# Batch 0's keys kept once, and a new hand order: a block-sparse attention and hardswish kernel on one core

## The chip, the cores and the metric

The kernel runs on one core of a Trainium2 chip. The metric is the device time of one execution in microseconds. A NeuronCore has five engines that run side by side: TensorE (PE; its weight loads are listed as PEld), VectorE (DVE), ScalarE (ACT), GpSimd (POOL) and SyncE (SP). POOL and SP also issue DMAs.

## The reference

```python
batch, n_heads, seq, head_dim = (4, 8, 768, 64); block, window = (32, 16)
k_sum = k.reshape(B, H, nb, block, D).max(axis=3)       # 24 block maxima of the keys
v_sum = v.reshape(B, H, nb, block, D).mean(axis=3)
mask_l = np.abs(pos[:, None] - pos[None, :]) < window
scores_l = where(mask_l, scale * q @ k.T, -1e9)
scores_s = scale * q @ k_sum.T + np.log(block)
a = softmax(concatenate([scores_l, scores_s], axis=-1))
attn = a @ concatenate([v, v_sum], axis=2)
x = attn.transpose(0, 2, 1, 3).reshape(B * S, H * D)     # 3072 x 512
h = x @ w_in                                             # 512 x 2048
out = (h * clip(h + 3, 0, 6) / 6) @ w_out                # 2048 x 512
```

Inputs and output are float32. The kernel multiplies in bfloat16.

## The kernel before, in words

**Attention.** 64 queries (a "tile" t, 12 per head) see 96 neighbouring keys (`WIN`) and the 24 block maxima: 120 columns (`KEYS`). Two heads make a pair p, of which there are four (`NP`); j is the head of a pair, on partitions 0 to 63 or 64 to 127. For every tile the stationary operand of the scores is a 128-column slot of `kb` that holds its 96 keys, the 24 maxima and 8 zeros. Neighbouring windows overlap, so a key stands in two slots, and each pair's maxima stand in twelve. ACT takes the exponential, DVE multiplies the band mask, and the values are products of the exponentials (120 rows) with `vaug`: 64 rows of V, 32 rows of "halo" (the neighbour's rows), 24 block sums and a column of ones for the denominator.

**Batch 0** is done a pair at a time as it arrives: `load_k` and `load_q` (POOL, casting to bfloat16), `k_step` (sixteen transposes on PE, a DVE maximum `red`, copies into `kaug` for half 1 and half 0, a broadcast of the maxima), `q_step`, `scores`, `vsum_first` (block sums of V by products with the indicator `ind`), `halo`. Half 0 of a pair is tiles 6 to 11, half 1 tiles 0 to 5. **Batches 1 to 3** are loaded ahead (`load_raw`, `load_nat`) and transposed on DVE or by DMA; `scores_all`, `vsum` and `values_half` work on them.

**The FFN** works on eight token tiles s of 384 rows (two a batch): `f1` makes two of sixteen column blocks of w_in per step (8 matmuls of 384 columns), ACT and DVE turn them into g; `f2` multiplies g by w_out (16 matmuls for 128 rows), copies and stores. Its matmuls take most of TensorE's time.

**The order** of all engines is written out by hand in the string `ORDER`, in tokens such as `k01.2:A`: tag, step of that tag, engine. Tags: K, Q, V, I, O loads of K, Q, V, w_in, w_out (batch, part); k, q transposes and copies (batch, pair); s scores; u sums of V; h halos; v values; F and G steps of `f1` and `f2` (token tile, part); c, e, z, f constants; w the rest of the keys of a batch; y a two-element POOL copy that holds back loads. `Plan.run` walks the tokens, assigns buffers, and sorts by planned begin; each engine's queue then is in that order. Where it plans that PE will wait in the first 27 us (`WARM`), `keep` puts in filler matmuls of 512 columns (line 983) so that the clock stays up. PSUM is three pairs of banks "S" and two banks "h".

## Time and profile before

| | |
|---|---|
| median of 3 runs | 214.84 us (214.73 to 215.09) |
| the profiled execution | 214.44 us, of which the span is 212.7 |
| busy time of PE, DVE, ACT, POOL | 205.3, 149.8, 110.6, 66.9 us |
| filler matmuls of line 983 | 21, 8.2 us busy |
| DMA | 25.01 MB, 121846 packets |

A row of a timeline has the start, the time it took, the engine, the line, the operation, output and inputs, how many in a row, and in brackets the idle time before and what ended it. A row of a group has busy time and mean ns of one, then idle time before. A row of a window has the stretch, its length, busy time of PE, PEld, DVE, ACT and POOL with counts, the granted clock of TensorE, DMA share and GB/s. A DMA row has the issuing queue, count, size and median time from issue to landing.

### The profile page before, as it was taken

To read this page: it belongs to the slowest core of one execution; us is meant where nothing else is said; L and a number is where in the kernel's file an instruction comes from. 1 tells how busy PE (TensorE), PEld (TensorE's weight loads), DVE (VectorE), ACT (ScalarE), POOL (GpSimd) and SP (SyncE) were. 2 spreads that over 40 slices of the span, in tenths; PEclk is the share of its full clock that TensorE was granted. 3 is DMA by queue.
4 is the path that set the end of the run, shared out by engine and by line. 5 is a ranking of instruction groups with operands and counts; after the bars stand their busy time and mean duration, and the time that the engine had idled before them with its cause. 6 is when DMAs were issued, how large, how long until landed. Compare 5 with 4: busy or idle time off the path is not lost.

```text
span 212.7 us, 4928 instructions
## 1 busy us (share of the span) xinstructions
PE 205.3 (97%) x2105; PEld 116.8 (55%) x2105; DVE 149.8 (70%) x238; ACT 110.6 (52%) x157; POOL 66.9 (31%) x81
## 2 busy tenths in 40 slices
PE   7969999999999999999999999999999999999994
PEld 2447686655446555555555556555464555555462
DVE  5788988999978897898568679981874347542102
ACT  5478856658299036836893045669501246531120
POOL 7999247345420029945973000000000000000000
PEclk9988999999999999999999999999999999999999
DMA  4999999999999659999999999901109002000242
GB/s 64 184 157 194 179 135 177 147 149 184 151 115 47 176 123 103 143 210 153 162 148 143 136 190 171 208 0 52 51 3 197 0 3 99 0 0 3 99 159 89
DMA packets 121846, 25.01 MB, mean 118 GB/s; under 512 B 112864, under 2 KB 118880, under 8 KB 121824
## 3 DMA queue, kind: packets, MB, share of 16 engines
q0 software_dynamic: 102336, 14.47, 108.0%
q1 hardware_dynamic: 19488, 10.23, 20.4%
q8 instruction: 16, 0.26, 0.5%
q14 instruction: 6, 0.05, 0.1%
HBM read 28.93 MB, written 6.29 MB: 166 GB/s over the span
## 4 chain that ended last, share of the span: by engine, by line
PE 90%; DVE 6%; ACT 2%; issue 0%; ACTq 0%; DVEq 0%
PE S L868 39%; PE h L890 29%; PE S L890 11%; PE S L784 3%; PE h L983 2%; PE S L658 2%; DVE vaug L502 2%; ACT kb L502 1%; DVE xn L837 1%; DVE at L641 1%; DVE kb L544 1%; PE h L517 1%; PE S L694 1%; DVE q L502 1%; DVE red L538 0%
## 5 line engine op out<-in xcount | busy, mean ns | idle before, releaser
L868 PE MATMUL S<-x,win 128*128 128x384 bf16 (+1 forms) x544 | 88.3, 317 | 0.0
L874 ACT ACTIVATE r<-S 128x768 f32<-128x768 f32 x64 | 51.3, 811 | 67.2 <-PE S L868 65.6
L876 DVE SCALAR_TENSOR_TENSOR g<-r,S 128x768 bf16<-128x768 f32 x64 | 59.6, 948 | 26.8 <-ACT r L874 26.1
L868 PEld LDWEIGHTS <-win 128*128 128x128 bf16 x544 | 51.2, 98 | 34.8 <-issue 0.2
L890 PE MATMUL h<-wout,g 128*128 128x512 bf16 (+1 forms) x288 | 67.4, 370 | 0.0
L890 PEld LDWEIGHTS <-g 128*128 128x128 bf16 x416 | 38.4, 98 | 38.6
L890 PE MATMUL S<-wout,g 128*128 128x512 bf16 (+2 forms) x128 | 25.8, 346 | 0.0
L664 ACT ACTIVATE at<-S 120x1024 bf16<-120x1024 f32 x18 | 17.5, 1031 | 4.3 <-PE S L658 4.2
L453 POOL DMA_DIRECT2D vaug<-in_v_dram x16 | 15.2, 955 | 8.1 <-DMA wout<-in_moe_w_out_dram 4.3
L666 DVE TENSOR_TENSOR at<-at,mask 96x1024 bf16<-96x1024 bf16 x18 | 11.9, 685 | 7.4 <-ACT at L664 7.2
L442 POOL DMA_DIRECT2D nat<-in_q_dram x8 | 10.5, 1318 | 7.1 <-issue 7.1
L442 POOL DMA_DIRECT2D nat<-in_k_dram x8 | 10.7, 1348 | 5.0 <-issue 2.3
L502 ACT COPY ot<-h 128x512 f32<-128x512 f32 (+1 forms) x14 | 7.9, 567 | 7.3 <-PE h L890 5.2
L502 DVE COPY ot<-S 128x512 f32<-128x512 f32 (+2 forms) x6 | 3.5, 577 | 11.2 <-PE S L890 11.2
L719 DVE TENSOR_REDUCE red<-kb 128x48 bf16<-128x1536 bf16 x6 | 10.5, 1744 | 0.0
L502 DVE COPY vaug<-vs 24x768 bf16<-24x768 bf16 x17 | 6.0, 354 | 3.4 <-ACT vs L502 3.0
L784 PEld LDWEIGHTS <-at 120*64 120x64 bf16 x336 | 6.1, 111 | 2.7 <-issue 1.6
L983 PE MATMUL h<-g 128*128 128x512 bf16 x15 | 6.1, 566 | 1.5 <-DVE g L323 1.5
L792 DVE TENSOR_TENSOR xm<-S,rc 128x768 bf16<-128x768 f32 x8 | 7.5, 955 | 0.1
L596 DVE STREAM_TRANSPOSE kb<-nat 128x768 bf16<-128x768 bf16 x8 | 7.4, 957 | 0.0
L784 PE MATMUL S<-vaug,at 120*64 120x65 bf16 x336 | 7.0, 196 | 0.3 <-ACT vaug L502 0.3
L637 ACT ACTIVATE at<-S 120x768 bf16<-120x768 f32 x8 | 6.3, 818 | 1.8 <-PE S L628 1.7
(100 smaller groups left out, 161.4 us busy)
## 6 DMA issues: line engine op xcount, KB each, us to landing
out_dram<-ot SPq DMA_DIRECT2D x19, 256.0 KB, 2.5
vaug<-in_v_dram POOLq DMA_DIRECT2D x16, 192.0 KB, 8.0
win<-in_moe_w_in_dram POOLq DMA_DIRECT2D x4, 512.0 KB, 11.2
wout<-in_moe_w_out_dram POOLq DMA_DIRECT2D x4, 512.0 KB, 17.3
nat<-in_k_dram POOLq DMA_DIRECT2D x10, 192.0 KB, 13.1
nat<-in_q_dram POOLq DMA_DIRECT2D x10, 192.0 KB, 8.1
out_dram<-ot SPq DMA_DIRECT2D x4, 224.0 KB, 2.7
nat<-in_k_dram POOLq DMA_DIRECT2D x6, 128.0 KB, 7.0
```

The costliest lines, as they stand in the source:

```text
L442: op("POOL", 1.35, over=0.01, fn=lambda src=src, name=name, hs=hs, ds=ds, rows=rows: nc.gpsimd.dma_start(out=raw[b % 2][name][rows], in_=s ...
L453: op("POOL", 0.945, lambda: nc.gpsimd.dma_start(out=o[BLK:WIN, lo:hi, 0:D], in_=rows[:, lo:hi]), w=[("v", b % 2, c)], dma=1.28, els=1536)
L502: {"ACT": nc.scalar.copy, "DVE": nc.vector.tensor_copy, "POOL": nc.gpsimd.tensor_copy}[eng](o, i)
L664: op("ACT", 1.02, lambda: nc.scalar.activation(odds[0:KEYS, :, w], X.slot[0:KEYS], AF.Exp, scale=scl), r=[X], w=[("atg", k)])
L666: op("DVE", 0.69, lambda: nc.vector.tensor_tensor(odds[0:WIN, :, w].rearrange("p j (t c) -> p j t c", c=QB), odds[0:WIN, :, w].rearrange(" ...
L719: nc.vector.tensor_reduce(red.slot[:].rearrange("x (p u e n) -> x e u p n", p=NP, u=NS, e=2)[:, e], w[:, n * e:n * e + n, BLK:WIN].rearran ...
L784: nc.tensor.matmul(X.slot[64 * c:64 * c + 64, e, (D + 1) * y:(D + 1) * (y + 1)], at[p][0:KEYS, j, t * QB:(t + 1) * QB], vaug[b % 2][0:KEYS ...
L868: nc.tensor.matmul(h.slot[:, f, lo * 128:hi * 128].rearrange("p (u c) -> p u c", c=128), w_in_sb[:, kt, (ft + f) * 128:(ft + f + 1) * 128] ...
L874: op("ACT", 0.81, lambda: nc.scalar.activation(r.slot[:], h.slot[:, :, 0:HALF], AF.Relu, bias=0.5, scale=1.0 / 6.0), r=[h], w=[r], alloc=r)
L876: op("DVE", 0.955, lambda: nc.vector.scalar_tensor_tensor(gt[s].slot[:, ft:ft + 2], r.slot[:], 1.0, h.slot[:, :, 0:HALF], op0=ALU.min, op1 ...
L890: nc.tensor.matmul(bank(o)[:, a:z], gt[s].slot[:, ft, ts * 128:(ts + 1) * 128], w_out_sb[:, ft, a:z], start=(ft == 0), stop=(ft == NFT - 1))
L983: nc.tensor.matmul(o, idle[:, 0:128], idle[:], start=True, stop=True)
```

## The change

For batch 0 the keys of a pair are kept once: 32 halo columns, 768 keys in order, 24 maxima. A tile's 96 keys are a slice of it, and the maxima get two products of their own per half (384 columns, one for each head), into rows 96 to 119 of the same PSUM tile. The maximum is written straight into its place, and the copies write each key once. The queries of half 0 stay in the order in which they were loaded, and the products read them with a stride.

With it comes more. K of pairs 1 to 3 of batch 0 is loaded in float32 by SP and cast by ACT and DVE (`load_wide_k`). POOL makes its masks first, then loads Q, K of pair 0 and V, and only then the wide queries. The block sums of V of batch 0 are made for two pairs at a time. Batch 3's block sums no longer come from TensorE: POOL loads V once more, a block to a row (`load_blocks`), and DVE adds (`sum_blocks`). POOL may copy halos and block sums (`ANY`): it has three copies of halos (batches 0 and 1) and ten of block sums. `scores_all` takes its tiles by half instead of by pair, half 1 first. The second half of batch 1 is transposed by PE (twelve transposes) instead of by DMA. The order is written anew. There are 15 filler matmuls instead of 21.

```diff
-K01.0 K02.0 Q010.0 c.2 Q000.0 c.1 K00.0 k01.0 c.0 e.4 z2.0:D c.9 e.1 f.0 e.2 c.4 c.7 c.8 e.0 k01.1 k01.3:D z0.0:A z1.0:A
+K01.0 K02.0 c.0 c.8 f.0 c.2 c.1 c.3 Q000.0 K00.0 Q010.0 c.4 c.9 C01.0:D V00.0 V03.0 V01.0 z2.0:A C01.1:A z1.0:A z0.0:A z3.0:D
...
+    ANY = ("ACT", "DVE", "POOL")
-    kaug = [kb[0][:, p * NQ:(p + 1) * NQ] for p in range(NP)]
+    keys = [kb[0][:, p * NQ:(p + 1) * NQ].rearrange("x t c -> x (t c)")[:, 0:BLK + S + NB] for p in range(NP)]
...
+    def load_wide_k(b, lo, hi):
+        plan.at(f"K{b}{lo}")
+
+        def raw_(p, n):
+            at_ = 2 * (p - 1) * RUN * D
+            return hards[0][0:RP].rearrange("p f c -> p (f c)").bitcast(F32)[:, at_:at_ + n * RUN * D].rearrange("p (h s d) -> p h s d", h=n, s=RUN)
+        op("SP", 0.4, lambda: nc.sync.dma_start(out=raw_(lo, 2 * (hi - lo)), in_=k[b, 2 * lo:2 * hi].rearrange("h (p s) d -> p h s d", s=RUN)),
+           w=[("kf", p) for p in range(lo, hi)], dma=0.95 * (hi - lo), kind="load")
+        for p in range(lo, hi):
+            plan.at(f"C{b}{p}")
+            for j in range(2):
+                op(EITHER, {"ACT": 0.59, "DVE": 0.68}, lambda eng, p=p, j=j: copy(eng, knat[:, 2 * p + j], raw_(p, 2)[:, j]),
+                   r=[("kf", p)], w=[("kn", p, j)])
...
-            src = bass.AP(tb.tensor, x[:, 8 * t0 - 4, 0].offset, [list(tb.ap[0]), [8, t1 - t0], [1, WIN // RUN], [RP, RUN]])
-            copy(eng, f[:, t0:t1, 0:WIN].rearrange("p t (a s) -> p t a s", s=RUN), src)
+            x = bank(T).bitcast(BF16)[:, 0:S].rearrange("p (s r) -> p r s", s=RUN)
+            o = keys[p][:, 0:BLK + S].rearrange("p (r s) -> p r s", s=RUN)
+            n, m = BLK // RUN, HALF // RUN
             if half:
+                copy(eng, o[:, n:m], x[:, 0:m - n])
+                copy(eng, o[:, 0:n], x[:, RP - n:RP])
+            else:
+                copy(eng, o[:, m:RP + n], x[:, m - n:RP])
...
-        op("DVE", 0.24, over=0.03, fn=lambda: nc.vector.tensor_copy(kaug[p][:, :, WIN:KEYS], red.slot[:, 0:NB].unsqueeze(1).to_broadcast([128, NQ, NB])),
-           r=[red], w=[("km", p)])
...
+        def asks(rows, lo, hi):
+            if half:
+                return qT[1][rows, p, lo * QB:hi * QB]
+            return qT[0][rows, p].rearrange("p (s c) -> p c s", s=RUN // 2)[:, lo * RP // HQ:hi * RP // HQ]
+
         def mms():
+            for i in range(HQ):
+                t = low(half) + i
+                for j in range(2):
+                    rows = slice(64 * j, 64 * j + 64)
+                    nc.tensor.matmul(X[p, half].slot[0:WIN, j, i * QB:(i + 1) * QB], keys[p][rows, t * QB:t * QB + WIN],
+                                     asks(rows, i, i + 1), start=not masked, stop=not masked or i == HQ - 1)
+            for j in range(2):
+                rows = slice(64 * j, 64 * j + 64)
+                nc.tensor.matmul(X[p, half].slot[WIN:KEYS, j, 0:HALF], keys[p][rows, BLK + S:], asks(rows, 0, HQ), start=not masked, stop=True)
...
-    def vsum_first(c):
+    def vsum_first(cs):
...
             for t in range(NQ):
+                for i, c in enumerate(cs):
+                    nc.tensor.matmul(bank(T)[BLK * i:BLK * i + BLK, 0:2 * D], ind[:, t], vaug[0][0:WIN, 2 * c:2 * c + 2, t, 0:D],
+                                     start=(t == 0), stop=(t == NQ - 1))
...
+    def load_blocks(b, c):
+        plan.at(f"B{b}{c}")
+        op("POOL", 0.8, lambda: nc.gpsimd.dma_start(out=rows_v(b, c), in_=v[b, 2 * c:2 * c + 2].rearrange("h (n r) d -> n h (r d)", r=BLK)),
+           w=[("vb", b, c)], dma=0.95, els=192, free=[(n, 0, g) for n in ("Kr", "Qr") for g in range(4)])
+
+    def sum_blocks(b):
+        plan.at(f"U{b}")
+        vs, n = Buf("vs"), D // 2
+        for h in range(2):
+            for lo in (0, n):
+                def go(h=h, lo=lo):
+                    x = both[0][:].rearrange("p u m -> p (u m)")[:, h * BLK * D:(h + 1) * BLK * D].rearrange("p (r d) -> p d r", r=BLK)
+                    nc.vector.tensor_reduce(total[:, h * D + lo:h * D + lo + n], x[:, lo:lo + n], axis=AX.X, op=ALU.add)
+                op("DVE", 1.22, go, r=[("vb", b, c) for c in range(NP)], w=[("vp", b, h, lo)])
+        op(EITHER, {"ACT": 0.265, "DVE": 0.25}, lambda eng: copy(eng, vs.slot[:], total[:]), r=[("vp", b, h, lo) for h in range(2) for lo in (0, n)],
+           w=[vs], alloc=vs)
+        spread(b, vs)
...
-                op(EITHER, {"ACT": 0.83, "DVE": 0.37}, over=-0.02, fn=lambda eng, c=c, x=x: copy(
+                op(ANY, {"ACT": 0.83, "DVE": 0.37, "POOL": 0.95}, over=-0.02, fn=lambda eng, c=c, x=x: copy(
...
-        if b:
+        if b > 1 or b and not half:
             op("SP", 1.3, lambda: nc.sync.dma_start(out=xt[s].slot[:].rearrange("p u k c -> p (u k) c"), in_=xm.slot[:], transpose=True),
```

The tokens of the new order on which the prediction's steps turn, with what stands between them left out:

```
... u1.0 G11.4:D ... u1.1:D u1.7:D u1.3:P ... u1.6:P K35.0 K22.0 K23.0 Q23.0 u1.8:P ... v10.0 v10.3 ...
... U3.2 ... U3.1 ... U3.0 ... U3.3 w3.3:D ... U3.4:A ... u3.7:P u3.6:P u3.3:P u3.4:P V33.0 V30.0 V31.0 u3.1:P V32.0 h32.0 v33.3 v33.0 ...
```

More of the change, by code (lines that the diff above doesn't have):

```diff
@@ L311 @@
     op = plan.op
-    DRAM = {"out": 0}
+    rows0 = {(c, x): Buf("rows") for c in range(NP) for x in range(2)}
     def eye():
@@ L676, in mms @@
             for t in range(NQ):
-                nc.tensor.matmul(bank(T)[WIN:128, 0:2 * D], ind[:, t], vaug[0][0:WIN, 2 * c:2 * c + 2, t, 0:D],
-                                 start=(t == 0), stop=(t == NQ - 1))
-        op("PE", mm(NQ, 2 * D), mms, form="sums", r=[("v", 0, c), ("vz", 0, c), "ind"], w=[T], alloc=T)
-        op(EITHER, {"ACT": 0.265, "DVE": 0.3}, over=-0.03, fn=lambda eng: copy(eng, vf[c][WIN:KEYS, :, 0:D], bank(T)[WIN:KEYS, 0:2 * D].rearrange("p (h d) -> p h d", h=2)),
+                for i, c in enumerate(cs):
+                    nc.tensor.matmul(bank(T)[BLK * i:BLK * i + BLK, 0:2 * D], ind[:, t], vaug[0][0:WIN, 2 * c:2 * c + 2, t, 0:D],
+                                     start=(t == 0), stop=(t == NQ - 1))
@@ new lines, in vsum_first, with spread_first @@
+        plan.at(f"u0{cs[0]}")
+        op("PE", mm(NQ, 2 * D), mms, form="sums", r=["ind"] + [(n, 0, c) for n in ("v", "vz") for c in cs], w=[T], alloc=T,
+           touch=[rows0[c, x] for c in cs for x in range(2)])
+        for i, c in enumerate(cs):
+            spread_first(c, i, T)
+    def spread_first(c, i, T):
+        plan.at(f"u0{c}")
+        op(EITHER, {"ACT": 0.265, "DVE": 0.3}, over=-0.03, fn=lambda eng: copy(
+            eng, vf[c][WIN:KEYS, :, 0:D], bank(T)[BLK * i:BLK * i + NB, 0:2 * D].rearrange("p (h d) -> p h d", h=2)),
@@ L926 @@
         scores(0, [(p, 0)])
-        vsum_first(p)
         for x in range(2):
```

204 lines of the change are left out of this document (105 added, 99 removed).

## Prediction

> **What bounds the kernel now.** I read the page's busy times and chain first, then the windows by stage, then TensorE's timeline over the first 36 us, since that is where the change works.
>
> ```profile
> span 212.7 us, 4928 instructions
> ...
> PE 205.3 (97%) x2105; PEld 116.8 (55%) x2105; DVE 149.8 (70%) x238; ACT 110.6 (52%) x157; POOL 66.9 (31%) x81
> ...
> PE 90%; DVE 6%; ACT 2%; issue 0%; ACTq 0%; DVEq 0%
> ```
>
> ```profile
> 10.00:15.00 5.00, 3.30 (x80) 2.38 (x80) 4.23 (x8) 3.75 (x10) 5.00 (x9) 0.91 2.43 158
> 15.00:20.00 5.00, 4.91 (x86) 3.65 (x85) 4.37 (x12) 4.41 (x10) 5.00 (x6) 0.75 1.81 181
> 20.00:25.00 5.00, 4.30 (x89) 2.88 (x89) 4.83 (x14) 4.02 (x8) 2.72 (x3) 1.00 1.88 181
> 25.00:30.00 5.00, 4.71 (x135) 4.08 (x129) 4.87 (x12) 3.63 (x6) 1.33 (x1) 1.00 2.61 151
> 30.00:208.00 178.00, 178.00 (x1651) 99.27 (x1648) 123.88 (x172) 89.80 (x119) 44.21 (x47) 1.00 1.24 112
> 14.00:16.00 2.00, 1.75 (x22) 1.23 (x22) 1.86 (x6) 2.00 (x8) 2.00 (x3) 0.51 2.41 159
> 16.00:18.00 2.00, 1.91 (x42) 1.43 (x41) 1.58 (x6) 1.46 (x3) 2.00 (x3) 0.63 2.09 175
> ```
>
> The columns are the stretch, its length, busy time of PE, PEld, DVE, ACT, POOL, granted clock, DMA share, GB/s. TensorE has no idle time from 30 to 208 us. So the time is: when TensorE becomes saturated, plus the matmul work left then, plus a short tail. Before 30 us it idles for want of DVE (4.2 to 4.9 us busy in each 5), and part of its busy time is filler matmuls.
>
> ```profile
> 1.53 4.45 PE L983 MATMUL h<-g 128*128 128x512 bf16 x10 [1.53 <-DVE g L323]
> 5.90 0.85 PE L517 MATMUL h<-ident,nat 96*64 96x96 bf16 x16
> 6.69 0.85 PE L983 MATMUL h<-g 128*128 128x512 bf16 x2
> 7.53 0.53 PE L517 MATMUL h<-ident,nat 96*64 96x96 bf16 x16
> 7.99 1.04 PE L983 MATMUL S<-g 128*128 128x512 bf16 x4
> ...
> 23.95 0.55 PE L754 MATMUL S<-vaug,at 120*64 120x65 bf16 x8
> ...
> 28.28 0.61 PE L868 MATMUL S<-x,win 128*128 128x128 bf16 x8
> ...
> 34.45 1.79 PE L868 MATMUL S<-x,win 128*128 128x384 bf16 x10
> ```
>
> The milestone is the first matmul of the second token tile (F10.0). Before, it follows eight of the ten matmuls in the last row, at 162 ns each: 34.45 + 1.30 = 35.75 us. By then all attention of batch 0 and five of the first tile's eight w_in column pairs are done. In the changed order exactly the same stands ahead of F10.0, so the two milestones can be compared directly.
>
> **Startup, step by step.** Durations used:
>
> ```profile
> L453 POOL DMA_DIRECT2D vaug<-in_v_dram x16 | 15.2, 955 | 8.1 <-DMA wout<-in_moe_w_out_dram 4.3 <-DMA nat<-in_q_dram 1.9 <-DMA nat<-in_k_dram 1.4
> ...
> L502 ACT COPY ot<-h 128x512 f32<-128x512 f32 (+1 forms) x14 | 7.9, 567 | 7.3 <-PE h L890 5.2 <-DMA out_dram<-ot 2.1
> ...
> L637 ACT ACTIVATE at<-S 120x768 bf16<-120x768 f32 x8 | 6.3, 818 | 1.8 <-PE S L628 1.7
> ...
> L538 DVE TENSOR_REDUCE red<-h 128x24 bf16<-128x768 bf16 x4 | 3.8, 941 | 1.6 <-ACT kb L502 0.9 <-PE h L517 0.7
> ...
> L502 DVE COPY q<-S 128x384 bf16<-128x384 bf16 x6 | 2.7, 485 | 0.1
> ...
> L544 DVE COPY kb<-red 128x288 bf16<-128x288 bf16 x4 | 2.6, 646 | 0.1
> ```
>
> ```profile
> 15.42 0.82 DVE L502 COPY q<-S 128x384 bf16<-128x384 bf16 x2
> ```
>
> ```profile
> nat<-in_k_dram POOLq DMA_DIRECT2D x1, 384.0 KB, 5.3
> nat<-in_k_dram POOLq DMA_DIRECT2D x1, 192.0 KB, 3.7
> ...
> vaug<-in_v_dram POOLq DMA_DIRECT2D x4, 192.0 KB, 6.5
> ...
> out_dram<-ot SPq DMA_DIRECT2D x19, 256.0 KB, 2.5
> ```
>
> 1. *K of pairs 1 to 3 by SP, in float32.* Issue near 1.0 us (no row; ACT's and DVE's first instructions start at 0.8 to 1.0). Landing: from 3.5 (the 2.5 of the 256 KB stores) to 5.1 us (POOL's 3.7 after 1.4); I take 4.5, nearer the stores with 384 KB to move. Pair 1's two casts run at once on ACT and DVE (0.57): its transposes start at 5.1 instead of 5.90. The 768 KB of pairs 2 and 3: 5.9 to 7.5, taken 6.9; then three casts in a row on ACT to 8.5. TensorE spends seven fillers there (0.43 us each while cold, as the ten in the 1.53 row, then half that), to 8.3. So pair 2's transposes come *later*, 8.3 instead of 7.53. If the cast DMA were as quick as before, this step would cost 0.8 us by itself.
> 2. *DVE chain of keys.* From 9.15: q copies of 0.35 to 0.4 (now contiguous, as the two at 15.42; the group's mean is 0.485), key copies 0.55 to 0.6 where whole blocks of 96 were written, three maxima of 0.94, the mask 0.4. The 0.65 us broadcasts of maxima (line 544, four of them) and four memsets are gone. The chain ends at 14.9 and the last half-0 scores at 15.3.
> 3. *Sums over V.* V now comes ahead of the wide queries: POOL's masks, three loads of 0.7 and four V issues of 0.955 end at 9.3, and 6.5 us to landing puts the last V at 15.5. Two groups of 24 matmuls replace four of 12, at 15.3 and 16.3. ACT finishes three exps (0.82, with some overlap) and two casts by 18.3; the first values close then. Before, values began at 23.95 us.
> 4. *From 18.3 TensorE is nearly the bound:* values of three tiles, half-1 queries and scores. F00.0 at 24.3 (28.28 before). But F00.0 no longer means all attention is done: 8.1 us of work and 0.9 of waits stand before F10.0, which gives 33.3. **The startup lead is 35.75 - 33.3 = 2.4 us.** The same reckoning on the old order gives F00.0 at 28.1 and F10.0 at 35.7, so its error is small where landings are known.
>
> **Matmul work added and removed.**
>
> ```profile
> L628 PE MATMUL S<-q,kb 64*128 64x64 bf16 x96 | 3.0, 211 | 1.5 <-ACT kb L502 0.9 <-DVE kb L544 0.5
> ```
>
> ```profile
> 18.12 0.84 PE L677 MATMUL h<-vaug,ind 96*32 96x128 bf16 x12
> ...
> 31.41 0.39 PE L809 MATMUL h<-ident,xm 128*128 128x128 bf16 x4
> ...
> 64.21 0.85 PE L694 MATMUL S<-vaug,ind 96*32 96x128 bf16 x48
> ...
> 65.00 2.76 PE L890 MATMUL S<-wout,g 128*128 128x512 bf16 x12
> ```
>
> - Block maxima: 16 new products of 384 columns on 64 rows. 162 ns each if a pair's two halves run side by side, as the 96 old 64-column products do (12 fill 0.28 us): 8 x 0.16 = 1.3 us, already in steps 2 and 4; 2.6 if they don't, of which half lies in step 4's saturated part (+0.6). Each group changes the weights' shape twice; no row shows that price. It lies between 0 and the 0.21 us that one such product takes from issue to end; I take 0.05, near the low end because rows of unlike form in the timeline follow each other without idle time. Eight changes in step 4: 0.4, at most 1.7. [...] I add **+0.6** for both.
> - Batch 3's 48 sums go (0.85 less 0.2 of latency, -0.65); twelve transposes of batch 1's second half come (three groups, 0.22 each, +0.66). Net 0.
> - Batch 3's sums become four DVE reductions of 1024 (about 1.2 us by line 538's rate, 4.8 in all), where DVE has room: 123.9 of 178 us busy. Fewer copies of V sums and halos stay on DVE. Taken as 0.
> - Tail: both orders end with sixteen 128-column matmuls, a copy and a store. 0.
>
> **GpSimd's new copies.** Nothing in the trace shows POOL copying such a tile.
>
> ```profile
> L442 POOL DMA_DIRECT2D nat<-in_k_dram x8 | 10.7, 1348 | 5.0 <-issue 2.3 <-DMA nat<-in_q_dram 1.7 <-DVE g L876 1.0
> ...
> L502 DVE COPY vaug<-vs 24x768 bf16<-24x768 bf16 x17 | 6.0, 354 | 3.4 <-ACT vs L502 3.0
> L502 ACT COPY vaug<-vs 24x768 bf16<-24x768 bf16 x7 | 5.8, 828 | 0.2
> L433 POOL DMA_DIRECT2D nat<-in_k_dram x6 | 5.4, 900 | 1.3 <-DMA vaug<-in_v_dram 1.1 <-issue 0.2
> ...
> L332 POOL TENSOR_SCALAR_AFFINE_SELECT g<-g 96x128 bf16<-96x128 bf16 x1 | 0.3, 290 | 0.1
> L340 POOL TENSOR_SCALAR_AFFINE_SELECT g<-g 96x16 bf16<-96x16 bf16 x1 | 0.2, 238 | 0.0
> ```
>
> Call one copy c. Low end: the two selects give 52 ns per 112 elements, so 0.23 + 768 x 0.46 ns = 0.6. High end: ACT's 0.83 plus two DVE copies of 0.35 met on the way, 1.5. I take 1.0, nearest ACT's row. Batch 1 is the tight place: after the sums (u1.0) POOL makes two copies, issues one L433 and three L442 loads (0.9 + 4.0), then makes a third copy, on which the values v10.0 wait. With 0.6 us from matmul to first copy: 5.5 + 3c = 8.5. TensorE has six w_out groups (0.865 by the 65.00 row), five scores, two values and three transposes meanwhile: 7.9. **+0.6**, with c = 0.6 to 1.5 giving 0 to 2.1. Batch 3 has four copies and then its V loads behind them; by the same steps the last load lands some 2 us ahead of its values.
>
> [...]
>
> **Sum.** Profiled execution 214.44 (span 212.7 and 1.7 around it): -2.4 + 0.6 + 0.6 = -1.2, so 213.2. The runs' median of 214.84 lies 0.4 above that execution; the forecast is 213.6. About 0.2% (0.43 us) is what a measurement can tell from no change.
>
> **Rivals.**
> - *Full lead* (0.14): copies near 0.6 and products side by side; 214.84 - 2.4 = 212.4. For it: POOL's short selects. Against: the shape changes.
> - *Clock drop in the saturated part* (0.14). The rows for 14 to 18 us show the clock halved for 3.4 us after 10 to 15 had TensorE at 3.30 of 5 busy; there it had slack. The new order is as thin from 11 to 13.4 us and around 17. If the drop falls on step 4, up to 1.7 us of work is lost: 215.3; if half of it, 214.5.
> - *Early landings late* (0.10). The SP loads at their late ends push pair 2 from 8.3 to 9.1, and V by as much: 1.0 to 1.5 us less lead, 214.6 to 215.1.
> - *Slower: GpSimd copies are slow* (0.16). From c = 1.55 the stall of 3c - 2.4 exceeds the lead less the shape changes (1.8) by more than can be measured. At c = 2.0 it is 3.6 at v10.0 and about 1.5 more ahead of batch 3's values, whose last V loads queue behind five copies: -1.8 + 5.1, 218.1; at 1.8, 216.5. For it: DVE is busy 124 of 178 us, so that copies will meet, and each copy has twelve separate pieces of 64 elements. Against: ACT's 0.83 for the same tile.
>
> **Numbers.** The forecast has 0.46. Faster: 0.40 of that, all of the full lead, 0.04 of the mixed rivals: 0.58. Slower: 0.16, plus 0.12 of the clock and landing rivals: 0.28. Same: 0.14. The range runs from just under the full lead, 212.2, to the mild slow-copy case, 216.5.
>
> **What would show it.** Right: F10.0 near 33.3; key transposes of pair 2 at 8 to 8.5; POOL copies of 0.9 to 1.2; a TensorE gap of about half a microsecond near 72 us before the values of line 842. Wrong: F10.0 after 34.8, a halved clock between 18 and 24, POOL copies above 1.6, or idle TensorE near 148 us waiting for V.

## The result, and the profile after

The changed kernel is slower: 222.06 us median of 4 runs (221.58 to 226.04) against 214.80, a ratio of 1.0328 (95% interval 1.0306 to 1.035). The forecast was 213.6 us, faster, in a range of 212.2 to 216.5. The profiled execution took 222.23 us, 7.79 more than the one before. Executions of one kernel differ in how many windows of halved TensorE clock they have (the changed kernel's four have a granted clock of 0.947 to 0.974); the ratios here leave disturbed ones out, and where one execution is meant its granted clock is given.

The page of the changed kernel (busy time and share of the span), and its windows over the startup (columns as before):

```profile
span 220.5 us, 4905 instructions
...
PE 210.5 (95%) x2079; PEld 118.9 (54%) x2079; DVE 153.6 (70%) x229; ACT 110.2 (50%) x156; POOL 78.5 (36%) x96
```

```profile
5.00:10.00 5.00, 3.04 (x47) 1.73 (x48) 3.66 (x9) 3.76 (x8) 5.00 (x7) 1.00 1.35 208
10.00:15.00 5.00, 4.87 (x76) 3.17 (x75) 4.51 (x11) 2.33 (x6) 3.80 (x5) 0.63 2.44 156
15.00:20.00 5.00, 5.00 (x44) 2.08 (x40) 1.65 (x7) 2.12 (x3) 0.00 (x0) 0.50 1.77 184
20.00:25.00 5.00, 5.00 (x77) 3.50 (x75) 2.51 (x6) 3.17 (x7) 1.88 (x3) 0.51 1.21 202
25.00:30.00 5.00, 4.91 (x108) 3.41 (x102) 4.65 (x11) 3.53 (x8) 4.91 (x7) 1.00 1.37 130
```

From 15 to 25 us TensorE is busy all the time and VectorE 1.65 and 2.51 of 5, where before it was 4.37 and 4.83. The bound of the startup has changed sides. The clock is halved from 11.25 to 24.9 us. That is four times 3.41 us; each such stretch is called a halved window from here on. Before, there was one, from 14.06 to 17.47. TensorE's timeline of the changed kernel:

```profile
5.68 1.69 PE L1047 MATMUL h<-g 128*128 128x512 bf16 x7
8.97 0.53 PE L539 MATMUL h<-ident,nat 96*64 96x96 bf16 x16 [1.61 <-ACT nat L524]
...
10.59 0.84 PE L644 MATMUL S<-q,kb 64*96 64x64 bf16 x12
11.36 0.81 PE L648 MATMUL S<-q,kb 64*24 64x384 bf16 x2
...
17.04 0.88 PE L644 MATMUL S<-q,kb 64*96 64x64 bf16 x12
17.84 0.81 PE L648 MATMUL S<-q,kb 64*24 64x384 bf16 x2
...
26.74 0.46 PE L644 MATMUL S<-q,kb 64*96 64x64 bf16 x12
27.12 0.33 PE L648 MATMUL S<-q,kb 64*24 64x384 bf16 x2
...
30.66 0.89 PE L926 MATMUL S<-x,win 128*128 128x128 bf16 x12
...
36.66 4.61 PE L926 MATMUL S<-x,win 128*128 128x128 bf16 x30
```

F10.0, the 73rd product of line 926, is the 21st of the last row. It starts at 39.48, where 33.3 was forecast and 35.75 was before. Line 644 is a half's 12 score products, line 648 its two with the maxima: half 0 at 10.59 and 17.04, half 1 at 26.74. In the kernel before a half has 12 products only, and they take 0.28 us from their start to the next start:

```profile
19.56 0.35 PE L628 MATMUL S<-q,kb 64*128 64x64 bf16 x12
19.84 0.50 PE L617 MATMUL S<-g,ident 128*128 128x384 bf16 x2
```

The 7.79 us fall into three parts: 3.73 ahead of F10.0, 3.11 between F10.0 and TensorE's last end, 0.95 behind that. The same three times for every kernel below, each in its one profiled execution (e_hold1 and e_hold2 build on e_c128p, e_best and e_nomax on e_kcont128):

| kernel | F10.0 | F10.0 to TensorE's end | end to span's end | halved windows up to 35 us |
|---|---|---|---|---|
| before | 35.75 | 173.91 | 3.05 | 1 |
| **after** | 39.48 | 177.02 | 4.00 | 4 |
| e_fill1: pause filled | 39.14 | 179.09 | 4.00 | 3 |
| e_fill2: and five fillers | 41.07 | 177.12 | 3.98 | 3 |
| e_keys: before, keys part alone | 40.48 | 174.32 | 3.04 | 1 |
| e_sums: after, sums on TensorE | 38.97 | 176.67 | 4.01 | 3 |
| e_cont: after, queries in order | 38.03 | 176.48 | 4.01 | 3 |
| e_c128: and 128 columns | 37.78 | 176.99 | 4.00 | 3 |
| e_c128p: and K by GpSimd | 37.29 | 179.28 | 3.41 | 3 |
| e_hold1: and three fillers | 33.85 | 178.01 | 3.43 | 0 |
| e_hold2: or eight | 35.79 | 177.24 | 3.44 | 0 |
| e_strq: before, stride alone | 38.88 | 174.25 | 3.04 | 3 |
| e_kcont128: e_keys, in order, 128 | 36.20 | 174.09 | 3.04 | 0 |
| e_best: and five fillers fewer | 37.17 | 175.24 | 3.04 | 1 |
| e_nomax: e_kcont128 less maxima | 37.60 | 174.08 | 3.05 | 2 |
| e_nofill: before, eight fillers fewer | 37.38 | 174.02 | 3.05 | 0, but half pace to 21 |
| e_mix1: e_hold1's startup, old order behind | 34.88 | 176.48 | 3.05 | 0 |
| e_mix: e_hold2's | 35.33 | 176.24 | 3.05 | 0 |

Two readings of this table need care. First, one execution differs from the next: the fillers behind pair 1's transposes start at 5.68 in the changed kernel, 6.06 in e_c128 and 6.39 in e_cont, although the loads ahead of them are the same. So a step of less than about 0.7 us in F10.0 is not shown by one execution each. Second, in e_fill1 and e_c128p one more window is halved later, at 112.6 to 116.1 and 111.6 to 115.0 us, right behind a pause of TensorE of 1.7 and 2.2 us; their second column holds both.

### The profile page after: what moved, and what is told of

Same layout as the page of the kernel before. It is cut to its first block, busy times and chain, and to the rows that moved or that the text cites. A ratio compares the mean times of both kernels' runs of the same rounds, so it can differ in the third digit from the quotient of the medians.

```text
span 220.5 us, 4905 instructions
## 1 busy us (share of the span) xinstructions
PE 210.5 (95%) x2079; PEld 118.9 (54%) x2079; DVE 153.6 (70%) x229; ACT 110.2 (50%) x156; POOL 78.5 (36%) x96
## 4 chain that ended last, share of the span: by engine, by line
PE 82%; DVE 10%; DMA 3%; ACT 2%; issue 1%; SPq 0%; DVEq 0%; ACTq 0%
PE S L926 35%; PE h L948 20%; PE S L948 13%; DMA g<-in_k_dram 3%; DVE at L689 3%; PE S L842 3%; DVE vaug L524 2%; PE S L644 2%; PE S L648 2%; DVE total L733 2%; DVE g L934 2%; PE S L681 1%; DVE red L776 1%; PE S L631 1%; PE h L700 1%; PE S L1047 1%
## 5 line engine op out<-in xcount | busy, mean ns | idle before, releaser
L926 PE MATMUL S<-x,win 128*128 128x384 bf16 (+1 forms) x544 | 89.9, 317 | 0.7 <-DVE g L934 0.6
L948 PEld LDWEIGHTS <-g 128*128 128x128 bf16 x416 | 38.6, 98 | 39.2 <-issue 0.5
L948 PE MATMUL h<-wout,g 128*128 128x512 bf16 (+2 forms) x272 | 59.2, 354 | 0.0
L948 PE MATMUL S<-wout,g 128*128 128x512 bf16 x144 | 33.1, 379 | 0.0
L524 POOL COPY vaug<-vs 24x768 bf16<-24x768 bf16 x9 | 7.7, 866 | 39.7 <-ACT vs L524 30.3
L524 ACT COPY ot<-h 128x512 f32<-128x512 f32 (+2 forms) x12 | 6.2, 517 | 10.3 <-PE h L948 8.4
L524 DVE COPY ot<-S 128x512 f32<-128x512 f32 x3 | 2.1, 692 | 10.8 <-PE S L948 10.8
L524 ACT COPY ot<-S 128x512 f32<-128x512 f32 x6 | 3.5, 587 | 11.6 <-PE S L948 11.4
L733 DVE TENSOR_REDUCE total<-nat 128x32 f32<-128x1024 bf16 x4 | 7.6, 1910 | 0.0
```

What stands on the lines that cost most here:

```text
L524: {"ACT": nc.scalar.copy, "DVE": nc.vector.tensor_copy, "POOL": nc.gpsimd.tensor_copy}[eng](o, i)
L733: nc.vector.tensor_reduce(total[:, h * D + lo:h * D + lo + n], x[:, lo:lo + n], axis=AX.X, op=ALU.add)
L926: nc.tensor.matmul(h.slot[:, f, lo * 128:hi * 128].rearrange("p (u c) -> p u c", c=128), w_in_sb[:, kt, (ft + f) * 128:(ft + f + 1) * 128] ...
L948: nc.tensor.matmul(bank(o)[:, a:z], gt[s].slot[:, ft, ts * 128:(ts + 1) * 128], w_out_sb[:, ft, a:z], start=(ft == 0), stop=(ft == NFT - 1))
```

## The experiments

**First four: clock, late load, keys part, sums.** Theory A: the four halved windows make the loss, and TensorE's pause of 1.61 us at 7.4 sets them off. Rival B: the late 768 KB of K do it whatever the clock. Rival C: the keys kept once cost it. The load of B, with its size and its time from issue to landing:

```profile
g<-in_k_dram SPq DMA_DIRECT2D x1, 768.0 KB, 6.5
```

```diff
+            n = {'k02.0': 13}.get(o.key, n)        # e_fill1: fillers ahead of k02.0, 13 instead of 7
```

> The changed kernel with 13 instead of 7 filler products ahead of the transposes of pair 2's K (k02.0), so that TensorE works through the 1.6 us in which it waited for that transfer; everything else is as it was. Theory A (the granted clock costs the startup): the clock is halved for 13.65 us because TensorE stood still at 7.4 to 9.0; without the pause the halved stretch begins later or is shorter by at least two windows of 3.41 us, F10.0 comes at 35 to 37 instead of 39.5, and the kernel takes 217.5 to 220. Rival B (the late transfer and the key chain behind it set the startup, the clock does not matter): F10.0 stays at 39.2 to 39.8 and the kernel at 221.5 to 222.5. If the halved stretch stays as long although the pause is filled, the pause is not its trigger.

Measured 225.83 us (222.13 to 229.4), ratio 1.0394 (1.0334 to 1.0454). The pause is gone, one halved window with it, and F10.0 moves by 0.34. A's trigger falls: the halved stretch begins 2.4 us later and then lasts three windows. F10.0 stays next to the 39.2 to 39.8 of rival B, which e_c128p tries below.

```diff
+            n = {'k02.0': 13, ..., 's000.0': 1, 's030.1': 2, 'u00.0': 2}.get(o.key, n)        # e_fill2
```

> The same 13 fillers and five more: one before the first scores of pair 0, two before the first block-maxima scores of pair 3, two before the second block sums; all 11.5 to 20 us. Theory A: if the small products of that stretch are what keeps the clock from coming back, five denser products inside it shorten the halved stretch further than 13 alone, F10.0 at 34 to 36.5, total 216.5 to 219. If the clock is not touched by them, they are 5 x 0.43 = 2.2 us of extra work where TensorE is bound: F10.0 later than with 13 alone by 1 to 2 us, total 1 to 2 us longer. Rival B: F10.0 39.2 to 41, total 221.5 to 224.

Measured 223.88 us (222.58 to 224.43), ratio 1.0425 (1.0384 to 1.0466). The clock came back for one window in the middle (0.84 from 15 to 20 us, 0.50 from 20 to 25), but F10.0 is at 41.07: these fillers cost more than they bring.

```diff
-                        keys = kaug[p][rows, t]
...
+                    nc.tensor.matmul(X[p, half].slot[0:WIN, j, ...], keys[p][rows, t * QB:t * QB + WIN], asks(rows, i, i + 1), ...)
...
+                nc.tensor.matmul(X[p, half].slot[WIN:KEYS, j, 0:HALF], keys[p][rows, BLK + S:], asks(rows, 0, HQ), ...)
```

> The kernel before with one part of the change alone: the keys of batch 0 kept once (spans as slices, products of their own with the block maxima, queries of a half by a stride), in the order, the loads and the copies of before. Rival C (this part costs the loss): the extra products and their change of shape fall into the startup, F10.0 at 37 or later instead of 35.75, total 216 or more. Theory A has the loss in the new order and not in this part: F10.0 35.2 to 36.0, total 213.8 to 215.2, with one halved window of 3.41 us as before; a gain of more than 1 us would say that the four copies of the maxima were on the path.

Measured 219.21 to 223.41 us in four runs. Two of them had a clock of 0.992 and took 219.21 and 219.54, where the kernel before took 214.39 at the same clock. F10.0 at 40.48 is *later than in the changed kernel*, with one halved window as before. So C holds. Its timeline and its window from 10 to 15 us show why:

```profile
10.51 0.84 PE L626 MATMUL S<-q,kb 64*96 64x64 bf16 x12
11.28 0.81 PE L630 MATMUL S<-q,kb 64*24 64x384 bf16 x2
...
18.54 0.46 PE L626 MATMUL S<-q,kb 64*96 64x64 bf16 x12
18.92 0.33 PE L630 MATMUL S<-q,kb 64*24 64x384 bf16 x2
19.19 0.46 PE L626 MATMUL S<-q,kb 64*96 64x64 bf16 x12
```

```profile
10.00:15.00 5.00, 4.37 (x79) 2.64 (x78) 2.72 (x6) 2.53 (x7) 5.00 (x9) 0.99 2.41 156
```

At a full clock half 0 takes 1.51 us from start to next start (10.51 to 12.02, where the next two products, of line 613, begin), half 1 only 0.65. The changed kernel at 17.04 has the same 0.88 and 0.81 at *half* the clock: these products do not go by the clock. What the two halves read differs in one thing: half 0's queries come by a step of 48 elements. That the products go at the pace of their reads is theory D.

```diff
+        vsum(b)            # e_sums: for batch 3 too, in place of load_blocks and sum_blocks, with the tokens of its sums and loads
```

> The changed kernel with the block sums of batch 3 back on TensorE, instead of four reductions of VectorE from a second load of V. The startup is untouched: F10.0 39.5. If the four reductions of 1.91 us are what makes TensorE wait 0.60 us at 143.3, that wait goes and the total is 220.8 to 221.8, with 0.65 us of TensorE's work added back, so 221.5 to 222.5 if the work is all on the path. A total above 222.8 says that the reductions paid.

Measured 222.05 us (221.34 to 226.79), ratio 1.0337 (1.0303 to 1.0371): no difference from the changed kernel. TensorE's wait of 0.60 us at 143.3 is gone, the sums are back. The startup is untouched, and yet this execution has one halved window less and F10.0 0.51 earlier.

**Next four: the pace of the reads, and the clock by itself.**

```diff
-        op(EITHER, ..., lambda eng: copy(eng, qT[0][:, p], bank(T)...[:, 0:HALF]), ...)
+        op(EITHER, ..., lambda eng: copy(eng, qT[0][:, p].rearrange("p (c s) -> p c s", s=m), ...), ...)
...
-            return qT[0][rows, p].rearrange("p (s c) -> p c s", s=RUN // 2)[:, lo * RP // HQ:hi * RP // HQ]
+            return qT[half][rows, p, lo * QB:hi * QB]        # e_cont
```

> The changed kernel with one thing undone: the copies of half 0's queries write them in query order, as before, and the score products read them one after the other instead of by a step of 48 elements. New theory D: the score products of batch 0 run at the pace at which their operands are read, not at the clock's; a pair's half 0 takes 1.51 us in the kernel with the keys part alone and its half 1 0.65, at the same granted clock, and the stride is the one difference that the reads have. Then the four half-0 groups fall from 1.5 to about 0.65 us each, F10.0 comes 2.5 to 3.5 us earlier (36.0 to 37.0) and the kernel takes 218.0 to 219.5. Theory A (the halved clock makes the loss): the groups stay near 1.5 us while the clock is halved, F10.0 stays at 39 to 39.5, total 221.5 to 222.5.

Measured 221.26 us (220.26 to 225.88), ratio 1.0294 (1.0232 to 1.0355). F10.0 moves by 1.45, not 2.5 to 3.5, and 0.94 against e_sums, which has three halved windows too. The groups did fall, but only as far as the halved clock lets them; in its timeline half 0 is now at the clock's pace:

```profile
16.95 0.69 PE L644 MATMUL S<-q,kb 64*96 64x64 bf16 x12
17.56 0.49 PE L648 MATMUL S<-q,kb 64*24 64x384 bf16 x2
```

The stride had hidden part of the clock's price.

```diff
-                        asks = qT[half][rows, p, i * QB:(i + 1) * QB]
+                        asks = ... if half else qT[0][rows, p].rearrange("p (s c) -> p c s", s=RUN // 2)[...]   # e_strq, in before
```

> The kernel before with the stride alone: half 0's queries stay as the transposes leave them, their copy is contiguous, and the 64-column score products read them by a step of 48 elements; keys, maxima, order and fillers as before. Theory D: a pair's 12 products of half 0 take 0.77 us instead of 0.28, four times, 2.0 us more of TensorE's time, of which some 1 us falls into its waits of 10 to 15 us, and each query copy on VectorE is 0.13 us shorter: F10.0 36.2 to 37.5, total 215.3 to 216.6. Theory A: groups of 0.28 us, F10.0 35.3 to 35.9, total 214.0 to 214.9.

Measured 218.53 us (216.35 to 220.58), ratio 1.0133 (1.0064 to 1.0202). The old kernel with the stride alone is slower, though all four runs also have two or more halved windows (clock 0.953 to 0.984). Half 0, then half 1, in its timeline:

```profile
10.47 0.82 PE L627 MATMUL S<-q,kb 64*128 64x64 bf16 x12
...
15.51 0.35 PE L627 MATMUL S<-q,kb 64*128 64x64 bf16 x12
```

The price is 0.76 us against 0.28 per group, as forecast, 1.9 us in all. Three halved windows from 21.7 us on come on top, so that F10.0 is 3.1 later. Read by a step of 48 elements, the 12 products take 2.7 times the time that they take on queries in order; what in the read costs that time no run shows.

```diff
-                    ... slot[0:WIN, j, ...], keys[p][rows, t * QB:t * QB + WIN], ...
+                    w = 128 if half else WIN
+                    ... slot[0:w, j, ...], wide[p][rows, t * QB:t * QB + w], ...      # e_kcont128: e_keys with e_cont's edit and this one
```

> The kernel before with keys of batch 0 kept once (as in the run of that part alone), but with half 0's queries in query order, and with 128 instead of 96 key columns as weights in the products of half 1 (the 32 columns beyond land in rows that the products of the maxima write over, or that nobody reads). Theory D: half 0's 12 products take 0.38 us as half 1's did, and the two of the maxima 0.27 instead of 0.74, so F10.0 is 3 to 3.5 us earlier than with the stride (37.0 to 37.6) and the total 215.6 to 216.8. If weights of 96 columns load more slowly than those of 128 (28 and 19 ns each in the rows of the weight loads), half 1's 12 products take 0.28 us and half 0's 0.38, and F10.0 is 0.3 to 0.4 earlier still. If the columns do not matter, both take 0.38.

Measured 214.92 us (214.66 to 215.51, ten runs), ratio 1.0004 (0.9985 to 1.0022): level with the kernel before, better than expected, and with a granted clock of 1.0 in all ten. Half 0 with 96 columns, half 1 with 128:

```profile
10.03 0.46 PE L628 MATMUL S<-q,kb 64*96 64x64 bf16 x12
10.41 0.33 PE L632 MATMUL S<-q,kb 64*24 64x384 bf16 x2
...
15.23 0.35 PE L628 MATMUL S<-q,kb 64*128 64x64 bf16 x12
15.51 0.33 PE L632 MATMUL S<-q,kb 64*24 64x384 bf16 x2
```

128 columns are *faster* than 96: 0.28 us from start to start against 0.38, and half 1 with 96 columns took 0.38 in e_keys (18.54 to 18.92). The weight loads, grouped by shape, of the kernel before and of e_keys:

```profile
L628 PEld LDWEIGHTS <-kb 64*128 64x128 bf16 x96 | 2.3, 107 | 2.9 <-ACT kb L502 1.0 <-DVE kb L544 0.8 <-issue 0.5
```

```profile
L626 PEld LDWEIGHTS <-kb 64*96 64x96 bf16 x96 | 3.7, 126 | 2.4 <-issue 1.3 <-ACT kb L506 0.8
```

The 96 narrow ones keep the loader busy 3.7 us, the wide ones 2.3. Why the narrow ones are slower no run shows.

```diff
+            n = {'k02.0': 0, 'q020.0': 0, 's020.1': 0, 's031.0': 0}.get(o.key, n)        # e_nofill, in before
```

> The kernel before without the eight filler products between 6.7 and 16 us (two, four, one and one); no operation of the computation is touched. It measures what the clock alone costs in the startup. Theory A: with TensorE idle there the clock is halved for two to four windows of 3.41 us, F10.0 at 38 to 40, total 217 to 219.5. Theory D: the halved windows cost 0.3 to 0.6 us each, since TensorE has slack there: F10.0 35.8 to 37.2, total 214.6 to 216.2.

Measured 216.33 us (215.71 to 221.24), ratio 1.0051 (1.0016 to 1.0087). Its timeline shows the old order at half pace until 21 us (sixteen transposes 0.84 instead of 0.53, covers 0.81 instead of 0.50; a cover is the two products of line 617, which put the mask into PSUM ahead of half 0's scores):

```profile
13.25 0.84 PE L556 MATMUL S<-ident,nat 96*64 96x96 bf16 x16
...
18.54 0.81 PE L617 MATMUL S<-g,ident 128*128 128x384 bf16 x2
...
22.01 0.50 PE L617 MATMUL S<-g,ident 128*128 128x384 bf16 x2
```

That is over 10 us more at half pace than before, and F10.0 moves by 1.63. So in the old order, where TensorE has slack and eight fillers less to work through, the clock is cheap in this execution, as D said. It is not so in every one: four of the ten, at clocks of 0.938 to 0.952, took 219.2 to 221.2 us, and none of them was profiled.

**Next four: repair, and price the rest.**

```diff
+                    w = 128 if half else WIN        # e_c128: e_cont with e_kcont128's columns
```

> The changed kernel with the queries of half 0 in query order and with 128 key columns as weights in the products of half 1. Theory D (pace of the reads and of the weight loads): half 1's groups of 12 take 0.28 us instead of 0.38; F10.0 comes 0.4 us before the 38.03 of the run with the queries alone, and the total is 219.6 to 220.6. What is left to the kernel before is then the four waits of TensorE between 5 and 12.5 us and the 10.2 us of halved clock that follow them. If the total stays at 220.3 to 220.6, the 128 columns buy nothing in this order; below 219 would say that the weight loads cost more than the rows show.

Measured 220.59 us (220.28 to 221.34), ratio 1.0272 (1.0242 to 1.0302). F10.0 is 0.25 earlier in one execution and the total is not: too little to be told from nothing here. The gain of 0.10 per group of half 1 is seen in the rows of e_kcont128.

```diff
-    load_wide_k(0, 1, 2)
+    load_k(0, 1, 2)          # e_c128p: and so for pairs 2 and 3, first in GpSimd's queue, without band; C01 to C03 go
```

> The same, and K of pairs 1 to 3 loaded by GpSimd with a casting transfer, first in its queue as before, instead of by SyncE in float32 with six casts on ScalarE and VectorE. Theory E (the late landing of the 768 KB and its casts hold the startup back): pair 2's transposes come at 7.6 to 8.3 instead of 9.4, TensorE's waits before 12.5 us shrink from 3.3 to under 1.5 us, the halved stretch is shorter by at least one window of 3.41 us, F10.0 at 35.5 to 37, total 217.5 to 219.5. Against it: V's loads then queue behind two more issues on GpSimd, 1.8 us; if V sets the startup, F10.0 stays at 37.5 to 39 and the total at 219.8 to 221.

Measured 219.40 us (215.94 to 222.62), ratio 1.0108 (1.0061 to 1.0156). Theory E: the late 768 KB and their casts hold the startup back. At clock 0.975 an execution took 218.93, where e_c128 took 220.46 at 0.974. Of these 1.5 us, 0.6 are the end behind TensorE (3.41 against 4.00, by the profiled executions), so that the float32 load with its casts is worth at most 0.9. Two executions at clock 1.0 took 215.94 and 216.69, 2.2 to 3.0 less than the one at 0.975: by these single executions, E explains part, and three halved windows cost that much in *this* order. The number of windows is not all: two executions at 0.992, one window by its clock, took 219.40 and 219.97.

```diff
+            n = {'q011.0': 0, 's031.0': 1, 'v00.0': 1}.get(o.key, n)        # e_best, on e_kcont128
```

> The kernel before with the keys part, queries in query order and 128 columns in half 1 (214.9 us), and without five of its filler products, at 13.3 to 16 and at 24 us, where TensorE had no idle time in that run. Theory D: five fillers of 0.22 to 0.4 us on a TensorE that is nearly the bound: F10.0 at 35.2 to 35.9 instead of 36.2, total 213.9 to 214.8, which is level with the kernel before or up to 0.7 us better. If the fillers held the clock up, a halved window appears and the total is 215 to 216.5.

Measured 217.10 us (215.8 to 219.24), ratio 1.0089 (1.0059 to 1.0118): worse. F10.0 is 0.97 later: without the five fillers a halved window falls on 27.1 to 30.55 us, where the FFN has begun. Another 1.15 us are lost behind F10.0, where this execution has a pause of 1.05 us at 109.1; that part is not shown to come from the fillers. Even the one execution at clock 1.0, 215.80, is above all of e_kcont128's.

```diff
-                nc.tensor.matmul(X[p, half].slot[WIN:KEYS, j, 0:HALF], keys[p][rows, BLK + S:], ...)        # e_nomax, on e_kcont128
+                    w = 128
```

> The kernel before with the keys part, queries in query order, 128 columns in both halves, and without the 16 products with the block maxima: the scores of the maxima are left out (their rows hold key columns), so this only prices those products. Their rows are 0.27 us per pair and half, 2.2 us in all, and half 0's 128 columns save another 0.4. Theory D, with TensorE nearly the bound from 10 to 28 us: F10.0 at 33.8 to 35.0, total 212.4 to 213.8, so the kept keys by themselves are worth 1 to 2 us and the products with the maxima spend it. If the landing of V or the copies hold the startup: F10.0 35.2 to 36.2, total 214 to 214.9.

Measured 217.08 us (215.57 to 218.09), ratio 1.0105 (1.0056 to 1.0155). This kernel leaves out the scores of the maxima. *Less* work, and F10.0 is 1.40 later. TensorE now waits, at 17.6 and 20.6 us, and two windows from 23.8 us on are halved, where it is bound (the waits, then the halved stretch):

```profile
PE h L678 <- DVE vaug L508: 1.4, 1, 1.4
...
PE S L678 <- DVE vaug L508: 1.1, 1, 1.1
```

```profile
23.70:30.50 6.80, 6.74 (x138) 5.54 (x138) 5.43 (x15) 4.58 (x7) 1.42 (x2) 0.51 2.53 156
```

**Two more: does the clock cause it, or go along with it?**

```diff
+            n = {'k00.0': 2, 's000.0': 1}.get(o.key, n)                                        # e_hold1, on e_c128p
+            n = {'k00.0': 2, 's000.0': 2, 's030.1': 2, 'u01.0': 2}.get(o.key, n)               # e_hold2, on e_c128p
```

> The kernel with contiguous queries, 128 columns in half 1 and K by GpSimd, and three more filler products: two before pair 0's key transposes (11 us) and one before pair 0's scores. Its executions without these ran from 215.9 us, where no window was halved, to 218.9 and more with three of them. If the halved windows cost 1 us each in this order, and TensorE's waits of 1.4 us between 9.3 and 12.7 us are their trigger, filling half of them takes away one to three windows: the fastest executions 216.2 to 217, the median 216.5 to 218.5. If the clock is only a companion, three products of 0.22 to 0.4 us are added to the path and the total is 216.7 to 220.5, spread as before.

> The same with eight more fillers in place of three: two before pair 0's key transposes, two before its scores, two before the scores of pair 3 and two before the first block sums (11 to 18 us). If dense products are what holds the clock, no window is halved and the total is 216.8 to 217.8, with little spread: the 215.9 of an undisturbed execution and eight products of 0.22 us, half of them in waits. If the small products around them decide it whatever is put between, three windows stay halved and the total is 220 to 222.

e_hold1: 219.02 us (216.99 to 219.65), ratio 1.0188 (1.0145 to 1.0232). e_hold2: 217.53 (216.54 to 218.17), 1.0119 (1.0079 to 1.0159), granted clock 0.997 to 1.0 in all five. The clock is a cause: in the profiled execution of e_hold1 no window is halved up to TensorE's end, and F10.0 comes at 33.85, 3.44 earlier than in e_c128p with three. In e_hold2, which has no halved window there either but five more fillers, it comes 1.50 earlier. Part of the distance between the two is their loads: the fillers behind pair 1's transposes start at 6.54 in e_c128p, 5.96 in e_hold1 and 7.02 in e_hold2. What the clock does is plain in one row: the same sums over V, in e_c128p and then in e_hold1:

```profile
18.27 1.47 PE L710 MATMUL h<-vaug,ind 96*32 96x128 bf16 x24
```

```profile
16.14 0.85 PE L710 MATMUL h<-vaug,ind 96*32 96x128 bf16 x24
```

Four of e_hold1's six executions still have one halved window (0.992) and take 218.9 to 219.7. They were not profiled, so whether it falls in the startup or behind the pause near 108 us, as in e_fill1 and e_c128p, is open.

**Last two: the order behind F10.0.** The new startup with the old order behind it, so with batch 3's sums on TensorE and batch 1's second half turned by DMA as before. e_mix1 has e_hold1's fillers, e_mix e_hold2's:

```diff
-... F03.2 F01.7 F03.3 F10.0 F10.1 F10.2 F13.0 ...
+... F03.2 F01.7 F03.3 F10.0 F02.0 ... F03.7 F10.1 F12.4 ...        # e_mix1, e_mix: from here the tokens of before
-        if b > 1 or b and not half:
+        if b:
```

> The startup of the changed order up to F10.0, with its three repairs (queries in query order, 128 columns in half 1, K by GpSimd) and three more fillers, and from F10.0 on the order of the kernel before, with batch 3's sums on TensorE and both halves of batch 1 turned by transfers as before. The step still open is the later order: in five runs with the order of before, 173.9 to 174.3 us lie between F10.0 and TensorE's end, in eight with the changed one 176.5 to 179.3, and the ends after it differ by 0.4 to 0.95. If that difference belongs to the later order, this kernel has F10.0 at 33.9, 174 us and an end of 3.1 to 3.4: 212.5 to 213.3 without a halved window, 214.5 to 215.3 with one, and so would beat the kernel before where the clock holds. If it comes with the earlier startup (loads of batch 1 that are then late), the 176.5 or more stay and the total is 215 to 217.

> The same with eight fillers more instead of three, which held the clock in all five executions of that startup: F10.0 at 35.8, 174 us behind it, total 214.2 to 215.0 if the later order is what the changed kernel loses behind F10.0, level with the kernel before; 217 to 218 if not.

e_mix1 216.80 us (216.1 to 218.27), ratio 1.0111 (1.008 to 1.0143); e_mix 216.73 (216.26 to 217.98), 1.0109 (1.0084 to 1.0134). Between the two answers: the end is back at 3.05, but 176.2 to 176.5 us remain behind F10.0. e_mix1's waits behind 30 us name part of it:

```profile
PE S L935 <- DVE g L943: 0.9, 2, 0.6
```

FFN steps that start earlier wait 0.9 us for VectorE; e_mix has the same two waits. So behind F10.0 e_mix takes 1.0 us less than e_hold2, and e_mix1 1.5 less than e_hold1, but both take 2.3 to 2.6 us more than the kernel before, of which 0.9 are these waits and the rest is open. The 1.0 and 1.5 cannot be credited to the old order: e_hold1's profiled execution has a pause of 1.67 us with no releaser, e_hold2's one of 0.44 us and a wait of 0.85 us for a load of V. The pause of e_hold1, and that of e_c128p:

```profile
107.34 0.20 PE L691 MATMUL S<-q,kb 64*128 64x64 bf16 x2 [1.67 <-issue]
```

```profile
111.03 2.23 PE L958 MATMUL h<-wout,g 128*128 128x512 bf16 x6 [2.23 <-issue]
```

No kernel beat the one before.

## Why the prediction was wrong

The profiled execution came out 9.0 us above the forecast for it, 222.23 against 213.24. Most of that is the startup: F10.0 at 39.48, not 33.3. Repaired step by step, each edit on top of the last, F10.0 moves by 1.45 (queries in order, and one halved window less), 0.25 (128 columns), 0.49 (K by GpSimd) and 3.44 (clock held by three fillers). That leaves 33.85, 0.55 from the forecast, with a quicker load of K than the forecast had. So the order of the startup was reckoned well; the prices in it were wrong. How much falls to the products and how much to the clock depends on the order of the edits: the stride hides part of the clock's price, and no run holds the clock with the strided queries.

- **The step that failed: "Matmul work added and removed", block maxima.** The sum had 1.3 us for 16 new products in steps 2 and 4, and +0.6 for the changes of shape and for products that do not run side by side: 1.9. Read in order, the two products of a half with their changes of shape take 0.27 us (18.92 to 19.19 in e_keys), 2.2 us for eight halves, so these prices were nearly right in sum; no run shows the change of shape by itself. Missing were two costs that the diff states: queries read by a stride, and weights of 96 columns. A pair's two halves went from 0.56 us to 2.16 (1.51 and 0.65), +6.4 us for four pairs. In the old order this part alone takes F10.0 from 35.75 to 40.48, and with the queries in order and 128 columns in half 1 to 36.20.
- **The rival "clock drop" was sized at one window, 1.7 us.** It was four, and the sign "a halved clock between 18 and 24" was seen. It was held less likely because there was slack where the one window fell before; in the new order TensorE is busy from 15 to 25 us, and three windows cost 2.2 to 3.4 us (e_c128p, e_hold1). What keeps the clock halved is not shown: the strided products are not needed for it, since e_c128, without them, still has three windows.
- **Step 1, K02.** The landing missed its range of 5.9 to 7.5: issued at 1.27, it landed 6.49 us later, at 7.76. The casts behind it took no longer than forecast (1.2 us from landing to transposes, where 1.4 was allowed), and pair 2's transposes came at 8.97, not 8.3, after 1.61 us of waiting. That is near the 9.1 of the rival "early landings late". From the chain of the changed kernel:

```profile
1.27 6.49 DMA g<-in_k_dram
7.78 1.15 ACT nat L524 x2
8.93 0.04 issue
8.97 0.55 PE h L539 x16
```

- **Steps 2 to 4.** With the clock held they come out close: in e_hold1 VectorE's last key copy ends at 14.8 (14.9 forecast), the sums begin at 16.14 (15.3) and the values at 19.05 (18.3). In the changed kernel the sums begin at 20.13.
- **GpSimd's copies.** c is 0.87, not 1.0, and TensorE has no wait for these copies: +0.6 was too much, and the rival with slow copies falls. Where copies of the two engines run beside each other they do lengthen, VectorE's from 0.35 to 0.89 us and GpSimd's from 0.82 to 1.01 at most. Groups of the changed kernel:

```profile
L524 POOL COPY vaug<-vs 24x768 bf16<-24x768 bf16 x9 | 7.7, 866 | 39.7 <-ACT vs L524 30.3 <-DVE vs L524 9.2
...
L733 DVE TENSOR_REDUCE total<-nat 128x32 f32<-128x1024 bf16 x4 | 7.6, 1910 | 0.0
...
L524 DVE COPY vaug<-vs 24x768 bf16<-24x768 bf16 x12 | 6.3, 523 | 0.3
```

  Its VectorE copies of the same tile take 523 ns on average where they took 354. In its trace eight of the twelve take 353 to 356 ns; the other four, which begin under a copy of GpSimd or just behind one, take 792 to 889. Of GpSimd's nine, the three that run beside such a copy take 845 to 1006 ns, the other six 819 to 827. That a copy of GpSimd takes the whole time of two copies of VectorE on top, as in the high end of 1.5, was an estimate; no run shows it.
- **Batch 3's sums, taken as 0.** The reductions are 1.91 us each, not 1.2, and a wait of 0.60 follows, yet e_sums, without them, is no faster: taken as 0 was right in sum, though one wait and one price in it were not foreseen.
- **Tail, taken as 0: 0.95.** The last section has the rows for it.
- **Behind F10.0, +0.6: 3.11.** Of these, 2.02 are these waits of the changed kernel:

```profile
PE h L746 <- ACT ot L524: 0.7, 1, 0.7
PE S L926 <- DVE g L934: 0.6, 1, 0.6
...
PE S L867 <- DVE qwide L850: 0.4, 1, 0.4
PE S L842 <- DVE at L689: 0.4, 1, 0.4
```

  Transposes less sums are +0.08, where 0 was forecast. The last 1.0 us goes with 14 more changes from one kind of product to another (96 instead of 82, counted in the traces), some 0.07 us each by division; that was not tried by itself.

The chances were 0.58 for faster and 0.28 for slower, and no rival had slower score products; the one with the clock was sized at one window. Treating "the products fill as the old ones did" as one answer for all eight groups left the largest price out.

## What to carry over

Price a matmul by all three of its streams: how the moving operand lies in memory (12 score products took 0.76 us by a step of 48 elements and 0.28 in order), how many columns the weights have (0.38 us with 96, 0.28 with 128), and only then columns of output. An edit that saves copies on the engine that waits may hand its cost to the bound: here 2.6 us of VectorE's copies became 6 us of TensorE's products. Where a startup is made tight, the clock must be planned with it. By an estimate from these runs, a us at half pace cost 0.16 us in the slack order (e_nofill: 1.63 us for some 10.3, and without the work of eight fillers) and 0.2 to 0.3 in the tight one (e_c128p and e_hold1: 2.2 to 3.4 us for 10.2).

## What was not expected of the hardware

- Up to 120 us, halved stretches in every trace are multiples of 3.41 us (one such window in the kernel before, from 14.06 to 17.47, and four in the changed one, from 11.25 to 24.9). A busy TensorE did not end them: 5.00 of 5 busy at clock 0.50 from 15 to 20 us in the changed kernel. With eight more fillers of 512 columns in the startup no window was halved up to 35 us (e_hold2).
- Taking work away put F10.0 later in two kernels (e_best, e_nomax), and in both a window was halved in front of it that e_kcont128 does not have.
- The profile's granted clock reads 1.00 in e_nofill from 5 to 21 us though the products show half pace (covers of 0.81 us at 18.54, of 0.50 at 22.01). In the kernel before it reads 1.00 from 0 to 7.2 us, where the first ten fillers start 0.43 us apart, and its record begins at 7.23. So a clock of 1.00 in a run that was not profiled does not rule out a slow start.
- The tail goes with the order in which SyncE waits for its stores at the end; no run changes that order alone. In the changed kernel the last store's semaphore stands second in that list, and seven more waits follow its landing; before, it was last. Times of the traces' landings and semaphore records, in us:

```
before: last landing 211.78; waits 116 at 211.25, 117 at 211.59, 118 (last store) at 211.79; drain 211.87
after:  last landing 218.67; wait 101 (last store) at 218.69, then 104, 113 to 118 until 219.59; drain 219.66
```

- Most kernels on the changed order, and e_best, have a pause of 0.4 to 2.2 us between 105 and 114 us, in a group of score products or right behind one, for which the profile shows no releaser. A 16 KB fetch of instructions begins 0.5 to 2.1 us ahead of it. But before, after and e_keys have such a fetch there too (at 107.3, 110.1 and 109.6 us) and no such pause. Its cause was not tried.
